# Attention and two mixture-of-experts layers in one kernel: the first layer's overflow loop moved into its routing, and the second expert's second matrix product turned around

## The chip, the cores and the metric

One Trainium2 chip, one of its NeuronCores. The metric is the device time of one execution of the whole kernel in microseconds (us), the median of a few runs. In the rows below PE is the matrix engine and PEld its weight loads, DVE the vector engine, ACT the scalar engine, POOL the general one, and SP the engine whose queue issues most of the transfers; a "q" behind a name (PEldq, SPq) means the engine's sequencer, which waits, branches and issues.

## What is computed

Top-32 attention over 16 heads, then two layers in which each of 1152 tokens goes through one of eight experts. Cut to what matters here:

```python
x = attention(q, k, v)                       # 1152 tokens, 512 wide
for w_gate, w1, w2, capacity in (moe, moe2): # capacity 288 in the first, none in the second
    logits = x @ w_gate
    expert_idx = np.argmax(logits, axis=1)
    for e in range(8):
        xe = x[expert_idx == e]              # the first 288 of them in the first layer
        h = np.maximum(xe @ w1[e], 0.0)      # w1[e] is 512x1024
        out[expert_idx == e] = gate_w * (h @ w2[e])   # w2[e] is 1024x512
    x = out
```

## The kernel before, in words

The program is attention, then the two layers (`moe(0, ...)` and `moe(1, ...)`), written out in one order by hand: no scheduler moves anything, and each engine takes its instructions as they are written.

A layer first routes its tokens. The experts are ranked by how many tokens chose them (rank r = 0 is the fullest), and rank r has room for `SIZES[r]` tokens: 256, 208, 192, 176, 160, 144, 128, 128. Tokens beyond that room go to an overflow loop, `spill()` (L1258): every engine loads the number of overflow blocks, `nblk`, into a register (L1259) and branches (L1261) over the loop's body if it is zero. With this input it is zero in both layers, so the loop itself never runs; what runs is the load and the branch on each engine. In the first layer `spill` stands in the last expert's layer 1 (`side`, L1422: with r == E - 1), ahead of `nxt.soon()`, the routing of the second layer. In the second layer it stands at the end of `run`.

The first layer's start is `begin()` (L1424). It ranks, then `assign()` (L1206) makes the token lists (`gidx`), runs 22 empty matmuls (`spin`), and computes the gate's parts (`r3`, L1228) and at last `nblk` (L1242). Then it asks for the first expert's w1 in four transfers of half a megabyte (`load_w1`, L872), gathers the first two blocks of rows (`bring`, L869), asks for w2 (`load_w2`, behind a POOL memset, L889), gathers further rows, turns the first rows (`turn_in`: PE transposes at L949, ACT at L952, DVE at L955) with 10 and 5 spins between, and asks for the second expert's w1 (`weights(1, 0)`). Each weight half (1 MB) lies in a `raw` buffer, of which there are four; a buffer comes free when ACT and DVE have split it into two parts (L919, L920: `halves`).

Then for each rank r: `layer1` over eight blocks f of the hidden width, with side work popped before each block f > 0 (the next expert's rows, the outputs of the last one, the splits of w2), and `layer2`. In both a matrix product takes three partial products. Forms: "D" and "R" issue three matmuls; "S" puts two of them into one matmul with 2n columns and adds them up after (ACT L971, DVE L972); "N" is plain. In layer 2, "R" keeps the hidden values in the array and streams w2 (512 columns), one pass for each block of up to 128 tokens (L1027 to L1029), and its result has tokens in rows: ACT scales it (L1075), and in the first layer PE turns it back for the next layer's logits (L1088). "S" keeps w2 in the array and streams the tokens (L1031, L1033); its result lies the other way, and PE turns it for the output (L1082). `form2` (L1108) gives rank 0 and 1 and the ranks of 128 the form "R", the others "S"; in the first layer the last rank has "N".

Of the kernel before, what the change touches and what calls it, by code (L numbers as in the profile page):

```python
# [10 lines left out]
F32 = mybir.dt.float32  # L11
F32R = mybir.dt.float32r
# [35 lines left out]
def attn_moe_moe_kernel(ctx, tc, q, k, v, g1, w11, w12, capacity, g2, w21, w22, out):  # L48
    nc = tc.nc
# [770 lines left out]
    def moe(i, pools, src, lg, w1, w2, limit):  # L820
# [4 lines left out]
        with ExitStack():  # L825
# [8 lines left out]
            width = Dm if i == 0 else RW  # L834
            ny = SIZES[0] if i == 0 else SIZES[2]
            xrs = {}
# [34 lines left out]

            def load_w1(e, first=0):  # L872
                w_ = w1[ds(e, 1)].rearrange("o (c p) f -> p (o c) f", p=128)
                got = []
                for h in range(2):
                    raw = wt.tile([128, KD, F // 2], F32, name="raw", bufs=4)
                    step = F // 4 if first else F // 2
                    for f0 in range(0, F // 2, step):
                        nc.sync.dma_start(raw[:, :, f0:f0 + step], w_[:, :, h * F // 2 + f0:h * F // 2 + f0 + step])
                    got.append(raw)  # L880
                return got
# [225 lines left out]
            form1 = ["D" if n >= 240 else "S" if n > 128 else "N" for n in SIZES]  # L1107
            form2 = ["R" if n >= 208 or n <= 128 else "S" for n in SIZES]  # L1108
            if i == 0:
# [101 lines left out]
            def assign():  # L1211
# [8 lines left out]
                if i == 0:  # L1220
                    spin(22)
                    for f in table["gates"]:
                        f()
# [3 lines left out]
                decode(pi[:, :NCOL], pi[:, NCOL:2 * NCOL], tokf, gidx, inv)  # L1227
                tt(r3, isa[:, None].to_broadcast(b3), gcode[:, :, None, :].to_broadcast(b3), op=OP.mult)  # L1228
                nc.scalar.activation(cnt, pos[:, nch], AF.Copy)
# [11 lines left out]
                red(nbf, more, axis=AX.XY, op=OP.add)  # L1241
                nc.vector.tensor_copy(nblk, nbf)  # L1242

            def weights(r, j):
                e = nc.values_load(eid0[0:1, 0:1] if i and r == 0 else eid[0:1, r:r + 1], engines=[SP], min_val=0, max_val=E - 1,
                                   skip_runtime_bounds_check_because="ranks are a permutation of the experts")
                if j == 0:
                    w1s[r] = [load_w1(e, sum(c[0] == 0 for c in COLS) if r == 0 and i == 0 else 0), {}]
                else:
                    w2s[r] = [load_w2_apart(e) if i == 0 and r == E - 1 else load_w2(e, r == 0), {}]  # L1250

# [6 lines left out]
            def spill():  # L1258
                trips = nc.values_load(nblk[0:1, 0:1], min_val=0, max_val=n_ov,  # L1259
                                       skip_runtime_bounds_check_because="a sum of block counts")  # L1260
                with ExitStack() as loop:  # L1261
# [53 lines left out]
                    red(g, pi[:, 2:5], axis=AX.X, op=OP.add)  # L1315
                    xr = wk.tile([128, width], F32, name="xr", bufs=5)
                    gather(xr, idx)
# [97 lines left out]
            def side(r, nxt):  # L1415
                jobs = opening() if r == 0 else []
                if r + 1 < E:
                    xTs[r + 1] = wk.tile([128, KD, 2, SIZES[0]], F32R, name="xT")
                    if r or i == 0:
                        jobs += [lambda q=q: rows_in(r + 1, *q) for q in tiles_of(r + 1)]  # L1420
                jobs += after(r - 1) if r else []
                return jobs + ([spill] + nxt.soon() if nxt and r == E - 1 else [])  # L1422

            def begin():  # L1424
                bank()
                choose(0, nch)
                count(0, nch)
                nc.scalar.activation(dl, dl, AF.Exp)
                none = new([128, 1], "none", U32)
                nc.gpsimd.memset(none, 0)  # L1430
                yr = wk.tile([128, RW], F32, name="yr", bufs=3)
                gather(yr[:16, :Dm], none[:16])
                spin(18)
                weave(*ranking())
                assign()
                weights(0, 0)
                for j in range(2):
                    bring(j)
                weights(0, 1)
                for a, (r, t, m) in enumerate(COLS):  # L1440
                    if 0 < r < 3:
                        bring(a)
                first_split = splits(0, 0)
                for f in first_split[:4]:
                    f()
                xTs[0] = wk.tile([128, KD, 2, SIZES[0]], F32R, name="xT")
                for q, n_ in zip(tiles_of(0), (10, 5)):
                    rows_in(0, *q)
                    spin(n_)
                for f in first_split[4:]:  # L1450
                    f()
                weights(1, 0)

# [122 lines left out]
            def run(nxt=None):  # L1576
# [3 lines left out]
                for r in range(E):  # L1580
                    hTs[r] = wk.tile([128, KF, 2, SIZES[0]], F32R, name="hT", bufs=1)
                    jobs, more_ = side(r, nxt), rest[r]
                    if i and r == 0:
                        more_ = [lambda p=p: [(split_high if p < 4 else split_low)(k) for k in w2_order[p]]
                                 for p in range(len(w2_order))]
                    jobs = [(lambda p=p: [f() for f in p]) for p in
                            [jobs[k:k + 1] + more_[k:k + 1] for k in range(max(len(jobs), len(more_)))]]
# [82 lines left out]
```

## Time and profile before

| | |
|---|---|
| median of 3 runs | 630.91 us (627.88 to 632.11) |
| the profiled execution | 628.57 us |
| its span, first to last instruction | 626.9 us |
| PE busy | 573.4 us, 91% of the span |
| granted TensorE clock, mean | 0.978 |

The attention fills the first 276 us; the change does not touch it. From about 276 to 296 us the first layer routes, from 296.4 to 455 us its experts run, the second layer's routing lies inside the last one, and from 468 to 619 us the second layer's experts run. In the rows, "idle before <- who" tells how long an engine sat idle and whose instruction ended that.

### The profile page before, as it was taken

The numbers are of one execution on the slowest core, as the hardware profiler recorded it, in microseconds if no ns is written. First come the engines' busy times: TensorE is split into PE (matmuls) and PEld (weight loads), VectorE is DVE, ScalarE is ACT, GpSimd is POOL, SyncE is SP. The second block draws the span as 40 slices with busy tenths as digits, with TensorE's granted clock in tenths as the row PEclk, the third lists the DMA queues.
The fourth block names the chain that finished last, engine by engine and source line by source line (L and its number), as shares of the span: only waits on it lengthen the run. The fifth ranks groups of instructions, "written<-read, shape, count | busy, mean of one in ns | idle before, by whom it ended". The sixth has DMA issues, their size and how long they took to land. (4 is left out here: it accounts for less than half of the span.)

```text
span 626.9 us, 13493 instructions
## 1 busy us (share of the span) xinstructions
PE 573.4 (91%) x4426; PEld 525.5 (84%) x4426; DVE 508.3 (81%) x1889; ACT 446.9 (71%) x963; POOL 242.6 (39%) x426
## 2 busy tenths in 40 slices
PE   7999989888888888676999999999899999999995
PEld 5888878777777777565988999999799889999994
DVE  6999999999999999975867688873368687888740
ACT  5699988888989897733776777763245577787651
POOL 8688776767675464634020101100013311101010
PEclk9699999999999999987999999999998999999998
DMA  6600605051550000009795758778185966677660
GB/s 149 155 4 1 196 1 146 2 134 24 137 78 20 2 20 1 20 21 315 268 280 195 230 202 244 225 240 287 31 308 178 331 237 230 224 259 266 221 223 19
DMA packets 79694, 96.01 MB, mean 153 GB/s; under 512 B 33829, under 2 KB 42533, under 8 KB 79616
## 3 DMA queue, kind: packets, MB, share of 16 engines
q1 hardware_dynamic: 74688, 84.07, 42.8%
q0 software_dynamic: 3728, 10.70, 5.3%
q8 instruction: 38, 0.62, 0.4%
q10 hardware_dynamic: 1200, 0.30, 0.2%
q14 instruction: 40, 0.33, 0.2%
HBM read 82.32 MB, written 13.22 MB: 152 GB/s over the span
## 5 line engine op out<-in xcount | busy, mean ns | idle before, releaser
L375 POOL TENSOR_TENSOR m<-s,r 128x576 f32<-128x576 f32 x71 | 100.8, 1420 | 54.7 <-ACT r L370 49.6
L402 PE MATMUL xb<-vx,pT 128*128 128x73 f32 (+1 forms) x800 | 95.4, 268 | 4.0 <-ACT xl L415 2.9
L402 PEld LDWEIGHTS xb<-vx,pT 128*128 128x128 f32 (+1 forms) x800 | 87.0, 180 | 8.2 <-ACT xl L415 4.3
L992 PE MATMUL pp<-xT,w1c 128*128 128x416 f32 (+4 forms) x320 | 93.3, 361 | 0.0
L920 DVE TENSOR_TENSOR w2c<-raw,w2c 128x512 fp32r<-128x512 f32 x112 | 74.4, 684 | 15.8 <-ACT w2c L919 15.4
L994 PE MATMUL pp<-xT,w1c 128*128 128x208 f32 (+4 forms) x320 | 77.9, 243 | 0.0
L919 ACT ACTIVATE w2c<-raw 128x512 fp32r<-128x512 f32 x112 | 67.0, 623 | 6.4 <-PE pp L1033 3.7
L920 DVE TENSOR_TENSOR w1c<-raw,w1c 128x512 fp32r<-128x512 f32 x96 | 60.5, 684 | 11.0 <-ACT w1c L919 10.4
L1031 PE MATMUL pp<-hT,w2c 128*128 128x384 f32 (+3 forms) x256 | 68.7, 350 | 0.0
L307 PE MATMUL sc<-qkT 128*128 128x288 f32 x256 | 51.2, 322 | 17.8 <-DVE cand L331 16.6
L343 DVE MAX8 top<-y 128x8 f32<-128x160 f32 x216 | 67.1, 311 | 0.1
L310 ACT ACTIVATE s<-sc 128x576 f32<-128x576 f32 x72 | 47.0, 653 | 22.2 <-PE sc L307 19.7
L307 PEld LDWEIGHTS sc<-qkT 128*128 128x128 f32 x256 | 36.4, 190 | 29.8 <-DVE cand L331 29.1
L1033 PE MATMUL pp<-hT,w2c 128*128 128x192 f32 (+3 forms) x256 | 61.3, 240 | 0.0
L994 PEld LDWEIGHTS pp<-xT,w1c 128*128 128x128 f32 x320 | 61.2, 191 | 0.2
L992 PEld LDWEIGHTS pp<-xT,w1c 128*128 128x128 f32 x320 | 60.2, 188 | 0.8
L971 ACT ACTIVATE t<-pp 128x192 f32<-128x192 f32 (+4 forms) x112 | 34.9, 311 | 35.9 <-PE pp L994 26.1
L385 PE MATMUL pt<-ident,kept 128*128 128x128 f32 x355 | 54.0, 283 | 4.2 <-ACT kept L379 3.4
L390 ACT ACTIVATE pT<-pt 128x640 f32<-128x640 f32 x71 | 50.1, 705 | 9.8 <-PE pt L385 8.6
L919 ACT ACTIVATE w1c<-raw 128x512 fp32r<-128x512 f32 x96 | 53.3, 621 | 4.3 <-DMA raw<-in_moe_w_dram 4.3
L379 ACT ACTIVATE kept<-m,nb 128x576 f32<-128x576 f32 x71 | 54.7, 771 | 1.4 <-POOL m L375 1.3
L370 ACT ACTIVATE r<-s,nb 128x576 f32<-128x576 f32 x71 | 54.5, 768 | 0.6 <-POOL nb L365 0.5
(317 smaller groups left out, 1429.5 us busy)
## 6 DMA issues: line engine op xcount, KB each, us to landing
raw<-in_moe_w_dram SPq DMA_DIRECT2D x60, 1024.0 KB, 6.0
out_dram<-zero SPq DMA_DIRECT2D x3, 768.0 KB, 3.8
y<-yr POOLq DMA_DIRECT2D x8, 256.5 KB, 4.5
kraw<-in_k_dram SPq DMA_DIRECT2D x8, 256.0 KB, 3.0
vraw<-in_v_dram SPq DMA_DIRECT2D x16, 128.0 KB, 2.8
vx<-in_v_dram SPq DMA_DIRECT2D x16, 128.0 KB, 2.8
raw<-in_moe_w_dram SPq DMA_DIRECT2D x4, 512.0 KB, 6.4
w2c<-in_moe_w_dram SPq DMA_DIRECT2D x4, 512.0 KB, 9.5
```

The lines of the kernel that those rows point to most:

```text
L307: nc.tensor.matmul(sc[:, w, :W2], l, r[:, w * W2:(w + 1) * W2], start=(n_ == 0), stop=(n_ == len(ops) - 1))
L343: ops.append(lambda w=w, cur=cur: nc.vector.max(w, cur))
L370: nc.scalar.activation(r, s, AF.Relu, bias=nb[:, 1:2], scale=-BIG)
L375: nc.gpsimd.tensor_tensor(m, s, r, op=OP.subtract)
L379: nc.scalar.activation(kept[k % 3][:, :S], m, AF.Exp, bias=nb[:, 0:1], scale=scale)
L402: nc.tensor.matmul(o, pT[:, c2, cols], z["v"][:, c2, hh], start=(c2 == 0), stop=(c2 == NC - 1))
L919: nc.scalar.activation(o[:, 0], src_, AF.Copy)
L920: nc.vector.tensor_tensor(o[:, 1], src_, o[:, 0].bitcast(F32), op=OP.subtract)
L992: nc.tensor.matmul(ph[:, :2 * n].rearrange("p (w n) -> p w n", w=2), w[f][:, 0, d], xT[:, d, :, :n], start=st, stop=False)
L994: nc.tensor.matmul(ph[:, :n], w[f][:, 1, d], xT[:, d, 0, :n], start=False, stop=sp)
L1031: nc.tensor.matmul(py[:, :2 * n].rearrange("p (w n) -> p w n", w=2), w[f][:, 0, o], hT[:, f, :, :n], start=st, stop=False)
L1033: nc.tensor.matmul(py[:, :n], w[f][:, 1, o], hT[:, f, 0, :n], start=False, stop=sp)
```

## The change

1. In the first layer `spill()` leaves `side` and is called in `begin()`, behind the gathers of the first two blocks of rows. The 22 spins of `assign` become 14, and 8 stand behind `spill`. The gate's parts (`r3`) are computed behind `nblk`. The loop's row buffer is taken from the `w2c` buffers.
2. The first expert's w1 is asked for in two transfers of 1 MB: the first half ahead of `assign`, the second behind `spill`, then w2 without the POOL memset.
3. The second expert's w1 is no longer asked for in `begin()`, but from the side work of the first expert's layer 1, ahead of its sixth block (f = 5), behind a DVE memset of the buffer. The splits of the first expert's w2, one ahead of each block before, now stand two, two and four ahead of the blocks 5, 6 and 7.
4. Rank 1 (208 tokens) has the form "S" in layer 2, in both layers.

```diff
-            ny = SIZES[0] if i == 0 else SIZES[2]
+            ny = SIZES[0] if i == 0 else SIZES[1]
...
-            def load_w1(e, first=0):
+            def load_w1(e, halves_=(0, 1), gate=None):
...
-                for h in range(2):
+                for h in halves_:
                     raw = wt.tile([128, KD, F // 2], F32, name="raw", bufs=4)
-                    step = F // 4 if first else F // 2
-                    for f0 in range(0, F // 2, step):
-                        nc.sync.dma_start(raw[:, :, f0:f0 + step], w_[:, :, h * F // 2 + f0:h * F // 2 + f0 + step])
+                    if gate:
+                        gate.memset(raw[0:1, 0, 0:1], 0.0)
+                        gate = None
+                    nc.sync.dma_start(raw, w_[:, :, h * F // 2:(h + 1) * F // 2])
...
-            form2 = ["R" if n >= 208 or n <= 128 else "S" for n in SIZES]
+            form2 = ["R" if n >= 240 or n <= 128 else "S" for n in SIZES]
...
-                    spin(22)
+                    spin(14)
...
-                tt(r3, isa[:, None].to_broadcast(b3), gcode[:, :, None, :].to_broadcast(b3), op=OP.mult)
+                if i:
+                    gate_rows()
...
                 nc.vector.tensor_copy(nblk, nbf)
+                if i == 0:
+                    gate_rows()
+
+            def gate_rows():
+                tt(r3, isa[:, None].to_broadcast(b3), gcode[:, :, None, :].to_broadcast(b3), op=OP.mult)
...
-                    w2s[r] = [load_w2_apart(e) if i == 0 and r == E - 1 else load_w2(e, r == 0), {}]
+                    w2s[r] = [load_w2_apart(e) if i == 0 and r == E - 1 else load_w2(e, i == 1 and r == 0), {}]
+
+            def first_weights(h):
+                w1s.setdefault(0, [[], {}])[0].extend(load_w1(chosen_one(0), (h,)))
...
-                    xr = wk.tile([128, width], F32, name="xr", bufs=5)
+                    xr = wt.tile([128, 2, Dm], F32R, name="w2c", bufs=12).bitcast(F32)
+                    xr = xr.rearrange("p a b -> p (a b)")[:, :width]
...
-                return jobs + ([spill] + nxt.soon() if nxt and r == E - 1 else [])
+                return jobs + (nxt.soon() if nxt and r == E - 1 else [])
...
                 weave(*ranking())
+                first_weights(0)
                 assign()
-                weights(0, 0)
                 for j in range(2):
                     bring(j)
+                spill()
+                spin(8)
+                first_weights(1)
                 weights(0, 1)
...
-                weights(1, 0)
...
+                    if i == 0 and r == 0:
+                        more_ = [lambda p=p, m=more_: [m[k]() for k in p] for p in
+                                 ((), (), (), (), (0, 1), (2, 3), (4, 5, 6, 7))]
+                        jobs.append(lambda: weights(1, 0, nc.vector))
```

Where instructions stand now. SP's queue in the first layer's start: `eid` is the first expert's number, `raw` a weight buffer. Before:

```order
L1245 TENSOR_LOAD eid
L879 ISA
L879 DMA raw<-in_moe_w_dram 128x4x256
L879 ISA
L879 DMA raw<-in_moe_w_dram 128x4x256
...
L1245 TENSOR_LOAD eid
L891 ISA
L891 DMA raw<-in_moe_w_dram 128x4x512
```

Now:

```order
L1252 TENSOR_LOAD eid
L880 ISA
L880 DMA raw<-in_moe_w_dram 128x4x512
L1272 TENSOR_LOAD nblk
L1274 COMPARE_AND_BRANCH x2
L1274 UNCONDITIONAL_BRANCH x2
...
L1252 TENSOR_LOAD eid
L880 ISA
L880 DMA raw<-in_moe_w_dram 128x4x512
```

The second half of w1, and all that SP issues after it, stand behind the branch now.

DVE from the fourth hidden block of the first expert's layer 1 to its layer 2: `hT` is a hidden block, `w2c` and `w1c` are splits. Before:

```order
L965 SCALAR_TENSOR_TENSOR hT<-pp,hT 128x256
L955 TENSOR_TENSOR xT<-pt,xT 128x4x80
L920 TENSOR_TENSOR w2c<-raw,w2c 128x512
L965 SCALAR_TENSOR_TENSOR hT<-pp,hT 128x256
L920 TENSOR_TENSOR w2c<-raw,w2c 128x512
...
L920 TENSOR_TENSOR w2c<-raw,w2c 128x512
L920 TENSOR_TENSOR w1c<-raw,w1c 128x512 x8
L920 TENSOR_TENSOR w2c<-raw,w2c 128x512 x3
```

Now:

```order
L966 SCALAR_TENSOR_TENSOR hT<-pp,hT 128x256
L878 MEMSET raw 1x1
L921 TENSOR_TENSOR w2c<-raw,w2c 128x512 x2
L966 SCALAR_TENSOR_TENSOR hT<-pp,hT 128x256
L921 TENSOR_TENSOR w2c<-raw,w2c 128x512 x2
L966 SCALAR_TENSOR_TENSOR hT<-pp,hT 128x256
L921 TENSOR_TENSOR w2c<-raw,w2c 128x512 x4
L966 SCALAR_TENSOR_TENSOR hT<-pp,hT 128x256
L921 TENSOR_TENSOR w1c<-raw,w1c 128x512 x8
```

All eight splits of w2 stand behind the fifth hidden block now, and the last hidden block behind all of them.

PE in the last expert's layer 1 of the first layer: L985 are its matmuls, L1088 and L1045 turn the last outputs back and make logits, L1163 is the second layer's first count. Before:

```order
L985 MATMUL pp<-xT,raw 128x128 x4
L1088 MATMUL pt<-ident,yr 128x128 x4
L985 MATMUL pp<-xT,raw 128x128 x4
L1045 MATMUL pl<-wg,yT 128x8 x4
L985 MATMUL pp<-xT,raw 128x128 x4
L1259 TENSOR_LOAD nblk
L1261 COMPARE_AND_BRANCH x2
L1261 UNCONDITIONAL_BRANCH x2
...
L985 MATMUL pp<-xT,raw 128x128 x8
L1163 LDWEIGHTS before
```

Now:

```order
L986 MATMUL pp<-xT,raw 128x128 x4
L1089 MATMUL pt<-ident,yr 128x128 x4
L986 MATMUL pp<-xT,raw 128x128 x4
L1046 MATMUL pl<-wg,yT 128x8 x4
L986 MATMUL pp<-xT,raw 128x128 x8
L1164 LDWEIGHTS before
```

The load and the branch are gone, and the count stands one block of matmuls earlier.

## Rows read from the trace of the kernel before

**Rows 1.** Page: busy time of each engine, share of span, instructions.

```profile
PE 573.4 (91%) x4426; PEld 525.5 (84%) x4426; DVE 508.3 (81%) x1889; ACT 446.9 (71%) x963; POOL 242.6 (39%) x426
```

**Rows 2.** By stretch: length, busy PE, PEld, DVE, ACT, POOL (instructions), clock, DMA share, GB/s.

```profile
284.00:292.00 8.00, 3.35 (x34) 2.87 (x34) 4.68 (x18) 2.30 (x4) 5.04 (x6) 0.82 0.99 323
...
490.00:600.00 110.00, 110.00 (x789) 104.83 (x788) 85.29 (x211) 81.42 (x205) 19.55 (x20) 1.00 0.73 253
```

**Rows 3.** Timeline of the last expert's layer 1: start, length, instruction, idle before.

```profile
444.08 1.14 PE L985 MATMUL pp<-xT,raw 128*128 128x128 f32 x8
444.26 0.17 DVE L1048 TENSOR_SCALAR lg<-pl 128x8 f32<-128x8 f32 x1 [8.12 <-PE pl L1045]
...
445.31 0.31 DVE L1151 TENSOR_REDUCE mx<-lg 128x19 f32<-128x152 f32 x1 [0.88 <-DVEq L1261]
...
446.70 0.32 DVE L1158 TENSOR_TENSOR oh<-revm,m 128x152 bf16<-128x152 f32 x1
447.80 2.02 PE L985 MATMUL pp<-xT,raw 128*128 128x128 f32 x16 [2.59 <-PEq L1261]
```

**Rows 4.** The branches' own instructions, from the views of lines L1261 and L719.

```profile
L1261 PEldq COMPARE_BRANCH  x2: 422/2140/3859, 443.8 to 615.6; - x2
...
L719 PEldq COMPARE_BRANCH  x1: 367/367/367, 275.1 to 275.1; - x1
```

**Rows 5.** Timeline of the first layer's start.

```profile
284.42 2.56 PE L1105 MATMUL pp<-idle,ones 128*128 128x256 bf16 x22
...
285.22 1.15 POOL L869 DMA_INDIRECT xr<-x,gidx  x1 [2.81 <-DMA raw<-in_moe_w_dram]
...
286.31 0.15 DVE L1242 CAST nblk<-nbf 128x1 int32<-128x1 f32 x1
...
291.63 1.09 PE L949 MATMUL pt<-ident,xr 128*128 128x128 f32 x4 [4.65 <-issue]
292.51 2.34 PE L1105 MATMUL pp<-idle,ones 128*128 128x256 bf16 x10
```

**Rows 6.** Busy time and granted clock in two single microseconds of that start.

```profile
288.00:289.00 1.00, 0.00 (x0) 0.00 (x0) 1.00 (x3) 0.53 (x2) 0.92 (x1) 1.00 1.09 385
291.00:292.00 1.00, 0.37 (x2) 0.40 (x3) 0.00 (x0) 0.00 (x0) 0.40 (x1) 0.50 0.92 260
```

**Rows 7.** Waits of SP's queue from 430 to 452 us: total, times, longest.

```profile
SPq L1261 <- SPq L1261: 8.7, 2, 8.3
```

**Rows 8.** Issue to landing of gathers (`gidx`), of w1's transfers (L879); timeline of SP.

```profile
DMA to landing us min/median/max: 3.2/6.1/8.2
...
DMA to landing us min/median/max: 4.9/5.3/15.9
...
289.37 10.51 SPq L879 DMA_DIRECT2D raw<-in_moe_w_dram  x2
```

**Rows 9.** First expert: its layer 1 and layer 2 by stretch; two DVE instructions there.

```profile
296.44:310.21 13.77, 13.45 (x115) 13.21 (x115) 11.99 (x31) 9.30 (x20) 1.94 (x3) 1.00 0.93 325
310.21:321.12 10.91, 10.91 (x51) 9.02 (x49) 8.21 (x14) 7.32 (x14) 1.25 (x2) 1.00 0.75 255
...
306.51 0.42 DVE L965 SCALAR_TENSOR_TENSOR hT<-pp,hT 128x256 fp32r<-128x256 f32 x1
307.02 0.69 DVE L920 TENSOR_TENSOR w2c<-raw,w2c 128x512 fp32r<-128x512 f32 x1
```

**Rows 10.** Layer 2 by stretch: first layer's rank 1 (R) and 2 (S), second layer's rank 1.

```profile
334.35:345.44 11.09, 11.09 (x51) 8.07 (x49) 7.92 (x15) 7.40 (x15) 1.31 (x2) 1.00 0.59 190
357.68:366.79 9.11, 9.11 (x67) 9.11 (x65) 8.27 (x18) 7.55 (x17) 0.00 (x0) 1.00 0.54 202
507.90:518.97 11.07, 11.07 (x50) 8.08 (x49) 7.92 (x15) 7.40 (x15) 1.01 (x1) 1.00 0.71 238
```

**Rows 11.** Timeline of PE where four transposes of an output stand between matmuls.

```profile
542.33 0.60 PE L1082 MATMUL pt<-ident,yT 128*128 128x128 f32 x4
542.68 0.41 PE L992 MATMUL pp<-xT,w1c 128*128 128x352 f32 x1
```

More of the change, by code (lines that the diff above doesn't have):

```diff
@@ L1242, in assign, with chosen_one, weights @@
                 nc.vector.tensor_copy(nblk, nbf)
-            def weights(r, j):
-                e = nc.values_load(eid0[0:1, 0:1] if i and r == 0 else eid[0:1, r:r + 1], engines=[SP], min_val=0, max_val=E - 1,
-                                   skip_runtime_bounds_check_because="ranks are a permutation of the experts")
+                if i == 0:
+                    gate_rows()
+            def gate_rows():
+                tt(r3, isa[:, None].to_broadcast(b3), gcode[:, :, None, :].to_broadcast(b3), op=OP.mult)
+            def chosen_one(r):
+                return nc.values_load(eid0[0:1, 0:1] if i and r == 0 else eid[0:1, r:r + 1], engines=[SP], min_val=0,
+                                      max_val=E - 1, skip_runtime_bounds_check_because="ranks are a permutation of the experts")
+            def weights(r, j, gate=None):
+                e = chosen_one(r)
                 if j == 0:
-                    w1s[r] = [load_w1(e, sum(c[0] == 0 for c in COLS) if r == 0 and i == 0 else 0), {}]
+                    w1s[r] = [load_w1(e, gate=gate), {}]
                 else:
-                    w2s[r] = [load_w2_apart(e) if i == 0 and r == E - 1 else load_w2(e, r == 0), {}]
+                    w2s[r] = [load_w2_apart(e) if i == 0 and r == E - 1 else load_w2(e, i == 1 and r == 0), {}]
+            def first_weights(h):
+                w1s.setdefault(0, [[], {}])[0].extend(load_w1(chosen_one(0), (h,)))
             def splits(r, j):
```

## Prediction

> **What bounds the kernel now.** I first read the page's list of engines: PE is busy 573.4 us, 91% of the span [rows 1]. Then the busy time by stretch, because a share is a mean over stages: among the experts PE is busy 110.00 of 110 us [rows 2], so there a part moves the end only if it gives PE less to do or makes it wait. The same view shows the opposite in the first layer's start: from 284 to 292 us PE works 3.35 of 8 us, while the DMA engines are full at 323 GB/s [rows 2]. Last I read the timeline in the places where the change cuts, to find PE's gaps and what ends them. Two matter. In the last expert of the first layer PE stands still 2.59 us, ended by its own branch at L1261 [rows 3]; and in the first layer's start it stands still 4.65 us, from the last spin at 286.98 (284.42 + 2.56) to the first transpose of gathered rows at 291.63 [rows 5]. Everything between 296 and 442 us is PE working without a gap that matters, so a gain or loss at either end passes to the end undiminished unless a transfer or a split comes late.
>
> My sum is against the profiled execution's own 628.57 us, of which 1.7 lie outside its span of 626.9. It stands 2.3 us (0.4%) below the median of the runs shown, 630.91; I put the difference that I work out onto the median.
>
> **Part 1a: the branch leaves the last expert.** Of the 2.59 us, what is late next? The branch also held up DVE: the logits are written at 444.26 + 0.17 = 444.43, but the second layer's first choice begins at 445.31, 0.88 later, and ends at 446.70 + 0.32 = 447.02 [rows 3]. Without the branch it ends at 446.14. PE has the block that ends at 444.08 + 1.14 = 445.22, then one more (half of the 2.02 us for sixteen matmuls, 1.0), and then the count, which needs that choice: 446.2. So PE waits about 0.1 us for it instead of 2.59, and what comes after the count starts more than 2.59 us earlier, as one block less stands ahead of it. I take 2.5 us. The ends: 2.75 if the chain after the count had itself been late, 0.9 if DVE's choice were all that mattered.
>
> **Part 1b: the branch enters the first layer's start.** It must wait for `nblk`, ready at 286.31 + 0.15 = 286.46 [rows 5], a little earlier now because the gate's parts move behind it. The 14 spins end before that: 284.42 + 14 x 0.116 = 286.05 (22 took 2.56). PE's branch took 3.859 us in the one place and 0.422 and 0.367 in the two others [rows 4]. That is the unknown. The two short ones and the long one are the same instruction, skipping a loop body; the long one is the copy of the loop that moves here, with the same body of matmuls, so I take the long price. With some 0.4 us for the load of the register, PE is free at 286.3 + 0.4 + 3.9 = 290.6. The 8 spins then cost 8 x 0.234 = 1.9 us at the lower clock (ten took 2.34 at 292.51) or 0.9 at the full one, so the first transpose comes at 291.5 to 292.5, against 291.63 now. [...] The work up to the first product is some 4.8 us now, nearly all at the lower clock; if the upper one comes back a microsecond and a half sooner, 1.3 us are saved. Ends for 1b: 1.3 faster, 0.8 slower; I take 0. The branch is thus hidden under the gathers' landing, at no gain: a stall of 4.65 us becomes one of 4.5 and eight more spins.
>
> [...]
>
> Behind the branch on SP's queue now stand the second half of w1, w2 and all later weights. At the old place SP stood at the branch 8.3 us, until its last transfer had landed [rows 7]. So here it will stand until the first half of w1 is in. Asked for at about 282, 1 MB should land at 287 to 288 (the median transfer of w1 takes 5.3 [rows 8]), hardly after `nblk` anyway. The second half then goes out near 288.3, some 5 us later than now, and lands by 294 to 295. It is first needed at the fifth of eight blocks of layer 1, past 303 (296.44 and half of 13.77 [rows 9]). Cost nothing.
>
> **Parts 2 and 3: the weights of the second expert.** They are now asked for from 289.37 on, the second of them when its buffer comes free near 299.5 [rows 8]. Afterwards DVE asks for both at its fifth hidden block, which ends at 306.51 + 0.42 = 306.9 [rows 9]. With 5.3 us the first lands at 312.2, and the other some 3 us behind it (1 MB at the 325 GB/s of that stretch [rows 9]), at 315.5. ACT and DVE want to split them when they are done with w2. DVE's list from 306.9: eight splits at 0.69 and three hidden blocks at 0.42 are 6.8 us, to 313.7. So the transfer is just in time. The first tile of layer 2 starts at 310.21 and needs the last split and the last hidden block at its eighth step, 4.8 us in (16 steps take 10.91 [rows 9], so 7 x 0.68), 315.0: 1.3 us to spare. In layer 2 of this expert DVE is busy 8.21 of 10.91 us now [rows 9]; the backlog of about 2.5 us fits into the 2.7 that are left. Cost nothing, cover nearly used up; if it fails, the price is in the third rival. The POOL memset that goes and the DVE one that comes are single elements.
>
> **Part 4: rank 1 in the form "S".** With "R" its layer 2 takes 11.09 us in the first layer and 11.07 in the second; rank 2 with 192 tokens takes 9.11 as "S" [rows 10]. In proportion to the columns, 208/192, "S" takes 9.87; a part of each matmul that does not grow would make it less, down to 9.4. I take 9.8: 1.3 us saved in each. The result has to be turned. Four transposes shift the matmul behind them by 542.68 - 542.33 = 0.35 us [rows 11]; two tiles cost 0.7. In the first layer that replaces the turning back of the rows, about the same, so 1.3 remain; in the second nothing went before, so 0.6 remain. Together 1.9 (ends 1.5 and 2.8). ACT and DVE get four additions each, as at rank 2, where DVE is busy 8.27 of 9.11 us and PE all the time [rows 10]; they hide them.
>
> **Sum.** 2.5 + 0 + 0 + 1.9 = 4.4 us faster: 624.2 from the profiled 628.57, and 630.9 - 4.4 = 626.5 on the median. That is 0.7%. About 1% (6.3 us) is what a measurement of this kernel can tell from no change, so the forecast is: within 1%, on the fast side.
>
> **Rivals.**
> (a) *The branch is short.* The two short rows speak for it, the long one of the same body against. PE would pass at about 287.2 and stand before the gathers instead: the first was issued at 285.22 and lands after 3.2 to 8.2, median 6.1 us [rows 5, 8], less than now perhaps, because 1 MB and not 2 lies ahead of it. With rows at 289.5 and little idle time the clock may not fall, and the 4.8 us of work become 2.6. Gain 3 to 4 us more: 623.0. [...]
> (b) *The gain at the last expert is taken by the routing chain.* The second layer's route is a chain of choice, count, choice and gather, and only its head was looked at here; if a gather's landing or DVE ends it, only the 0.88 us of DVE remain. PE's unbroken work after the count speaks against. Total 0.9 + 1.9 = 2.8: 628.1.
> (c) *The second expert's weights come late; slower than before.* Place: the first expert's layer 2 and the second's layer 1. Both halves of w1 and then w2 are asked for inside 10 us, w1 up to 17.5 us later than now, from DMA engines that are at 255 to 325 GB/s there [rows 9]. Against: those rates include this very traffic, which is not yet there. One transfer of w1 took 15.9 us from issue to landing [rows 8]. If that came again from 306.9, it would land at 322.8, ACT and DVE would have split a first block at 324.2 (two steps of 0.69), and PE, due at 321.1, would lose 3.1 us there, and as much again with w2 one stage on: 6.2. The sum becomes 1.8 slower: 632.7. It decides from a loss of 4.4 us on, that is, 2.2 a stage, a landing 15.0 us after the request.
>
> **How the numbers follow.** Forecast 0.58 (its own range 624.0 to 628.5 by the ends of 1a, 1b and 4 and the spread of the median), (a) 0.17, (b) 0.16, (c) 0.09. The range for all reaches from case (a) with a little more, 621.5, to just short of (c), 631.0; the few runs of before alone span 4 us. Faster by over 1% is most of (a) and a fifth of the forecast, 0.26; slower by over 1% is the far end of (c), 0.04; within 1% 0.70.
>
> **What would show each step.** In the profile after: PE's idle time before the branch's successor in the last expert gone, and the count waiting at most some 0.3 us; PE's branch in the first layer's start with 3.9 us (forecast) or 0.4 (a); the first product at 295 to 297.3; no idle time of PE between 310 and 345 (else c); rank 1's layer 2 at 9.8 us. The prediction is wrong if the first product comes before 294, if PE waits for `w1c` of the second expert, or if the time is above 631.

## The result and the profile after

| | before | after |
|---|---|---|
| median of 4 runs each | 630.62 us (627.88 to 632.11) | 623.83 us (622.67 to 625.12) |
| the profiled execution | 628.57 us, span 626.9 | 624.27 us, span 622.6 |

The ratio is 0.990 (95% interval 0.986 to 0.994): 6.8 us faster by the medians (3.9 to 9.0 by the interval), 4.3 by the two profiles. A second comparison of the same two kernels, below, has 626.85 against 630.12 us, ratio 0.993 (0.991 to 0.996): 3.3 us by the medians, 4.3 by the ratio. The forecast was 4.4 us, 626.5, which lies inside both intervals. The total was met; two of its terms were not. The 623.83 is nearer to rival (a)'s 623.0, but that rival's condition, a short branch, did not come: the branch is long in the rows below.

The list of engines on the page of after, which answers to [rows 1]:

```profile
PE 571.0 (92%) x4466; PEld 528.1 (85%) x4466; DVE 510.7 (82%) x1898; ACT 447.3 (72%) x969; POOL 240.6 (39%) x425
```

The timeline of the last expert in after, for [rows 3]:

```profile
443.81 2.03 PE L986 MATMUL pp<-xT,raw 128*128 128x128 f32 x16
443.99 0.17 DVE L1049 TENSOR_SCALAR lg<-pl 128x8 f32<-128x8 f32 x1 [8.22 <-PE pl L1046]
444.19 0.31 DVE L1152 TENSOR_REDUCE mx<-lg 128x19 f32<-128x152 f32 x1
...
445.59 0.32 DVE L1159 TENSOR_TENSOR oh<-revm,m 128x152 bf16<-128x152 f32 x1
...
445.95 0.23 PE L1164 MATMUL pi<-oh,before 128*128 128x168 bf16 x1
```

The 2.59 us in front of PE are gone. DVE begins its choice 0.03 us behind the logits instead of 0.88, is done at 445.91, and PE's count starts 0.11 us behind the block that ends at 445.84: the forecast's 0.1.

The branches' instructions (line L1274 now) and the timeline of PE in the first layer's start, for [rows 4] and [rows 5]:

```profile
L1274 PEldq COMPARE_BRANCH  x2: 341/2056/3770, 287.0 to 611.2; - x2
```

```profile
284.82 1.69 PE L1106 MATMUL pp<-idle,ones 128*128 128x256 bf16 x14
290.95 1.87 PE L1106 MATMUL pp<-idle,ones 128*128 128x256 bf16 x8 [4.44 <-PEq L1274]
292.61 1.06 PE L950 MATMUL pt<-ident,xr 128*128 128x128 f32 x4
293.46 2.34 PE L1106 MATMUL pp<-idle,ones 128*128 128x256 bf16 x10
```

The long jump has moved with the loop: 3.770 us (3.859 before), a stall of 4.44 (forecast 4.5), then eight spins at 1.87 us, 0.23 each at the lower clock, where the fourteen ahead of the stall took 0.12 each. The first transpose comes 13.60 us behind the first count (279.01) instead of 13.03 (278.60). Busy time and granted clock there, for [rows 6]:

```profile
288.00:289.00 1.00, 0.00 (x0) 0.00 (x0) 0.00 (x0) 0.00 (x0) 0.48 (x1) 1.00 0.85 221
290.00:291.00 1.00, 0.05 (x1) 0.09 (x2) 0.00 (x0) 0.00 (x0) 0.69 (x2) 0.53 0.58 182
292.00:293.00 1.00, 1.00 (x6) 0.88 (x5) 1.00 (x3) 1.00 (x3) 0.00 (x0) 0.50 0.98 362
```

As in the kernel before, the granted clock falls from 1.00 to 0.50 while PE stands.

Last the stretches of after for [rows 9] and [rows 10]: the first expert's layer 2, the second expert's layer 2 in the first and in the second layer, and the last expert's layer 1 in the second layer.

```profile
310.87:322.07 11.20, 11.20 (x50) 9.02 (x49) 9.67 (x17) 8.05 (x16) 1.25 (x2) 1.00 1.05 392
601.23:609.26 8.03, 7.33 (x65) 7.14 (x64) 4.26 (x11) 4.37 (x12) 0.99 (x1) 1.00 0.08 28
```

```profile
335.31:344.91 9.60, 9.60 (x66) 9.59 (x65) 8.74 (x18) 7.63 (x17) 0.00 (x0) 1.00 0.54 196
...
503.07:512.66 9.59, 9.59 (x66) 9.57 (x65) 8.74 (x18) 7.62 (x17) 0.00 (x0) 1.00 0.67 236
```

Form S takes 9.6 us where R took 11.1, in both layers. The last expert's layer 1 in the second layer has 0.70 us in which PE isn't busy. The timeline shows why:

```profile
601.23 2.84 PE L986 MATMUL pp<-xT,raw 128*128 128x128 f32 x24
601.96 2.19 ACT L920 ACTIVATE w2c<-raw 128x512 fp32r<-128x512 f32 x4 [2.12 <-SPq L1274]
...
604.05 0.67 ACT L1076 ACTIVATE yr<-pp,gate 128x512 f32<-128x512 f32 x1
...
604.77 4.73 PE L986 MATMUL pp<-xT,raw 128*128 128x128 f32 x40 [0.70 <-ACT yr L1076]
```

ACT did this work in the order in which it is written: it waited 2.12 us for the last half of w2, split it, and only then, at 604.05, copied the output (yr) whose buffer PE needed. (The row names SP's branch; the transfer was asked for at 595.82 and landed 6.1 us later, at 601.9. The same transfer took 5.1 us in the kernel before.)

### The profile page after: what moved, and what is told of

Same layout as the page of the kernel before. It is cut to its first block, busy times and chain, and to the rows that moved or that the text cites. A ratio compares the mean times of both kernels' runs of the same rounds, so it can differ in the third digit from the quotient of the medians.

```text
span 622.6 us, 13581 instructions
## 1 busy us (share of the span) xinstructions
PE 571.0 (92%) x4466; PEld 528.1 (85%) x4466; DVE 510.7 (82%) x1898; ACT 447.3 (72%) x969; POOL 240.6 (39%) x425
## 4 chain that ended last, share of the span: by engine, by line
PE 39%; DMA 8%; issue 4%; DVE 1%; POOLq 0%; POOL 0%; ACT 0%
PE pp L993 8%; DMA out_dram<-yr,sidx 8%; PE pp L1032 7%; PE pp L995 3%; PE pp L1034 3%; PE pp L986 2%; PE pt L950 2%; PE pp L1030 2%; PE pp L1028 2%; PE pp L1029 1%; PE pl L1046 1%; PE pp L990 1%; PE pp L1026 1%; PE pp L989 1%; PE pp L991 1%
## 5 line engine op out<-in xcount | busy, mean ns | idle before, releaser
L921 DVE TENSOR_TENSOR w2c<-raw,w2c 128x512 fp32r<-128x512 f32 x112 | 74.2, 685 | 17.4 <-ACT w2c L920 17.3
L1032 PE MATMUL pp<-hT,w2c 128*128 128x416 f32 (+4 forms) x320 | 88.0, 354 | 0.0
L1034 PE MATMUL pp<-hT,w2c 128*128 128x208 f32 (+4 forms) x320 | 78.4, 245 | 0.0
L921 DVE TENSOR_TENSOR w1c<-raw,w1c 128x512 fp32r<-128x512 f32 x96 | 60.9, 687 | 11.1 <-ACT w1c L920 10.8
L972 ACT ACTIVATE t<-pp 128x208 f32<-128x208 f32 (+4 forms) x120 | 37.5, 313 | 40.6 <-PE pp L995 28.9
L1034 PEld LDWEIGHTS pp<-hT,w2c 128*128 128x128 f32 x320 | 61.3, 192 | 0.0
L1032 PEld LDWEIGHTS pp<-hT,w2c 128*128 128x128 f32 x320 | 60.2, 188 | 0.0
```

The lines of the kernel that those rows point to most:

```text
L921: nc.vector.tensor_tensor(o[:, 1], src_, o[:, 0].bitcast(F32), op=OP.subtract)
L1032: nc.tensor.matmul(py[:, :2 * n].rearrange("p (w n) -> p w n", w=2), w[f][:, 0, o], hT[:, f, :, :n], start=st, stop=False)
L1034: nc.tensor.matmul(py[:, :n], w[f][:, 1, o], hT[:, f, 0, :n], start=False, stop=sp)
```

## The experiments

Ratios are to the kernel before on the same chip, which had medians of 630.12, 629.62 and 630.74 us in the three groups.

| kernel | median, us | ratio, 95% interval |
|---|---|---|
| b_again: before | 629.29 | 0.999 (0.997 to 1.001) |
| a_again: after | 626.85 | 0.993 (0.991 to 0.996) |
| b_form2: before, with S | 628.70 | 0.998 (0.996 to 1.000) |
| a_oldform: after, with R | 625.93 | 0.992 (0.990 to 0.995) |
| a_form_first: S in layer one alone | 625.39 | 0.993 (0.990 to 0.995) |
| a_pad: after, jump shifted | 625.20 | 0.993 (0.990 to 0.995) |
| a_no8: after, no spins there | 625.87 | 0.993 (0.991 to 0.996) |
| b_pad: before, jump shifted | 627.40 | 0.995 (0.993 to 0.998) |
| a_spillback: part 1 undone | 629.19 | 0.998 (0.996 to 1.000) |
| a_oldw1: part 3 undone | 624.94 | 0.991 (0.988 to 0.993) |
| a_xrback: buffers as before | 625.26 | 0.991 (0.989 to 0.994) |
| best: three edits | 623.98 | 0.991 (0.988 to 0.994) |

The intervals are some 1.5 us to either side, so most verdicts rest on stages. Each profile's stages, in us, worked out from its timeline (from PE's first matmul of one stage to that of the next): the last expert's layer 1 and its whole time in the first layer; the start, from the first count to the second expert; the second layer's first expert; there rank 1's layer 2 up to rank 3; and its last expert up to the end of the span.

```
               last, L1   last   start   2nd: rank 0   1 to 3      end
before            12.48  27.45   42.52         29.05   30.23 R   20.41
b_again           13.84  28.79   41.78         29.08   30.23 R   20.46
b_form2           15.18  29.99   42.33         27.59   30.84 S   20.46
a_spillback       13.94  29.30   41.45         29.07   31.39 S   20.59
b_pad             10.56  26.50   42.59         29.07   30.23 R   20.38
after              9.94  24.60   43.06         27.31   29.67 S   21.38
a_again            9.94  24.61   43.01         27.65   31.23 S   21.70
a_oldform          9.93  24.67   42.97         27.62   30.38 R   20.56
a_form_first       9.93  24.58   43.19         27.64   30.55 R   20.76
a_pad              9.94  24.60   42.24         27.31   31.33 S   21.31
a_no8              9.94  24.60   41.95         29.17   31.05 S   20.51
a_oldw1            9.93  24.59   42.68         29.07   31.11 S   21.47
a_xrback           9.93  24.59   41.95         27.30   31.29 S   21.75
best               9.94  24.61   42.20         27.31   30.57 R   21.47
```

**Both kernels again** (b_again, a_again; no edit).

> The kernel before, unchanged, to see how its executions differ among themselves. In its first profile the granted clock falls to 0.50 from 480.21 to 483.62, right behind the second layer's short products (28 and 14 columns); in the profile after, there is no such stretch, and that alone is 2.0 of the 4.3 us between the two profiles. Theory A (chance): where that stretch falls differs from run to run; the mean clocks of these runs differ by about 0.003 among themselves (3.4 us at half speed in 627), and the times by some 1.8 us with each 0.003; another profile may lack the stretch. Theory B (the change removes it): every run of this kernel has it, mean clock 0.978 or lower throughout, and this profile shows it again.

> The changed kernel, unchanged, for the same question. Theory A: some of these runs have the low stretch in the second layer's start, clocks spread over 0.977 to 0.983; at equal mean clock it is 4.3 us faster than the kernel before by the terms (2.85 at the last expert, 1.97 from the form, less 0.56 in the first layer's start), and the ratio is near 0.993. Theory B: no run has the stretch, mean clock 0.980 or higher throughout, and the ratio is near 0.990 (some 6.3 us).

Neither theory held whole. The unchanged before had the low stretch in the second layer again (rank 0: 29.08 us), and a low stretch that was not expected, right behind the stall at the branch. Its windows around the stall, and the timeline:

```profile
446.00:447.50 1.50, 0.00 (x0) 0.00 (x0) 1.33 (x5) 0.00 (x0) 0.00 (x0) 1.00 0.05 5
448.00:451.00 3.00, 2.83 (x13) 2.87 (x14) 0.00 (x0) 0.28 (x1) 0.00 (x0) 0.50 0.02 5
452.00:454.00 2.00, 2.00 (x30) 2.00 (x28) 1.23 (x9) 0.28 (x1) 0.00 (x0) 1.00 0.00 0
```

```profile
448.17 3.47 PE L985 MATMUL pp<-xT,raw 128*128 128x128 f32 x16 [2.50 <-PEq L1261]
```

Sixteen matmuls that took 2.02 us in [rows 3] take 3.47 here, at clock 0.50: the stall did not cost 2.5 us but 3.9.

**Part 4 alone, and all but part 4.**

```diff
-            form2 = ["R" if n >= 208 or n <= 128 else "S" for n in SIZES]
+            form2 = ["R" if n >= 240 or n <= 128 else "S" for n in SIZES]
```

(a_oldform the other way round.)

> The kernel before with the second expert's layer 2 in the form S alone (part 4). Theory A: rank 1's layer 2 takes 9.6 to 9.8 us in both layers instead of 11.1, 0.15 us go to the turned output in the first layer and 0.85 in the second; 1.97 us faster, ratio 0.9969. The forecast's term is 1.9. Rival: the additions on ACT and DVE hold PE up somewhere in the next expert, and less than 1 us remains. The PE stall of some 2.6 us at the branch in the last expert is unchanged.

> The changed kernel with the second expert's layer 2 in the form R again (part 4 undone). Theory A: 2.0 us slower than the changed kernel, so 2.3 faster than before, ratio 0.996. Theory B (the low stretch of the clock in the second layer goes because the last expert runs through): 4.3 faster than before, ratio 0.993, and the profile has no low stretch at 475 to 480.

The first layer did as forecast: from rank 1's layer 2 to rank 3 it takes 31.13 us in b_form2 and 32.44 before, 1.3 less. In the second layer S took 30.84 against 30.23: the gain had gone. By the times part 4 made 1.3 us in the one comparison (0 to 2.6), and undoing it cost nothing that can be measured in the other: its interval excludes theory A's 0.996 and has theory B's 0.993 in it. Theory B's reason is not shown by that, as the low stretch in the second layer comes and goes in either kernel (rank 0 in the table). For the last expert, b_form2 shows the stall and the lower clock once more, longer:

```profile
445.00:451.00 6.00, 5.07 (x34) 5.04 (x35) 0.08 (x1) 0.55 (x2) 0.00 (x0) 0.50 0.01 3
```

Where the second layer's gain goes is seen in a_again: its two S stretches (rank 1 and rank 2), and the timeline inside the first.

```profile
505.73:516.10 10.37, 10.16 (x66) 9.55 (x65) 9.86 (x22) 8.01 (x18) 0.00 (x0) 1.00 0.61 211
...
527.00:536.96 9.96, 9.65 (x66) 9.20 (x65) 8.23 (x18) 7.55 (x17) 0.28 (x1) 1.00 0.71 239
```

```profile
507.68 0.38 ACT L965 ACTIVATE hT<-s 128x208 fp32r<-128x208 f32 x1 [0.38 <-DVE s L973]
...
507.98 0.46 PE L1032 MATMUL pp<-hT,w2c 128*128 128x416 f32 x1 [0.21 <-DVE hT L966]
508.08 0.37 DVE L966 SCALAR_TENSOR_TENSOR hT<-s,hT 128x208 fp32r<-128x208 f32 x1 [0.16 <-ACT hT L965]
...
508.61 1.90 DVE L921 TENSOR_TENSOR w1c<-raw,w1c 128x512 fp32r<-128x512 f32 x3
```

Some seven steps into layer 2, PE comes to the last hidden blocks before ACT and DVE have written them. S reads a step's hidden block in 0.30 us (9.6 for 32), R reads the same list for one tile first, in 5.5 us or so (half of 11.07 [rows 10]) for eight blocks, 0.69 each. The faster form reaches the last hidden block sooner, at the point where DVE is just done with layer 1.

That alone does not make PE wait: in the profile after, with the same form, there is no such wait, and the stretch took 29.67 us, 0.56 less than with R, about the 0.6 of the forecast. What sets it apart stands earlier, in rank 1's layer 1. Below is ACT's third copy (t) there, first of a_again with the last matmul that it needs, then of after:

```profile
499.63 0.26 PE L995 MATMUL pp<-xT,w1c 128*128 128x208 f32 x1
...
501.65 0.34 ACT L972 ACTIVATE t<-pp 128x208 f32<-128x208 f32 x1 [2.11 <-PE pp L995]
```

```profile
497.33 0.34 ACT L972 ACTIVATE t<-pp 128x208 f32<-128x208 f32 x1 [0.45 <-PE pp L995]
```

In a_again ACT begins 1.76 us after that matmul's end (499.89), in after 0.10; its hidden blocks are late from there on. Each of the seven S profiles with the long stretch has such an idle time of ACT in that layer, of 1.4 to 2.1 us, and a second one of 1.4 us where rank 2's layer 2 begins; after has 0.45 and 0.56 us there. Five of the six R profiles have the first one too, and PE waits for no hidden block there. So, by these profiles, S loses its gain where ACT is late, and R, which asks later, does not. What held ACT is not shown; whether it also happens without the profiler is not known.

**S in the first layer alone.**

```diff
-            form2 = ["R" if n >= 240 or n <= 128 else "S" for n in SIZES]
+            form2 = ["R" if n >= (208 if i else 240) or n <= 128 else "S" for n in SIZES]
```

> The changed kernel with the form S for the second expert in the first layer alone, R again in the second. Theory A (the second layer gives the gain back: its stretch from rank 1's layer 2 to the end took 119.0 us with R, and 119.5, 119.8 and 121.4 in three executions with S, with PE waiting there for hidden blocks and for an output's copy): that stretch is 119.0 to 119.4 us, no wait of PE for hT or yr there, and the kernel is 0.1 to 2 us faster than the changed one. Theory B (by the forecast, S saves 0.6 us in the second layer): 0.6 us slower than the changed one.

The stretch is 30.55 us, and of PE's waits for hT none is left; up to the end it took 119.80 from rank 1 on, above the 119.4 expected and above the 119.5 of after. In all, the six profiles with R in the second layer have 30.2 to 30.6 there, those with S 29.67 once and 30.84 to 31.39 seven times. Theory A holds for this stretch, at 0.6 us on the mean (30.99 less 30.37), and not up to the end; by the runs no gain is resolved.

**The place of the jump in PE's code.** Empty matmuls, nothing else:

```diff
                 choose(0, nch)
+                spin(20, 64)
                 count(0, nch)
...
-                spin(18)
+                spin(36, 128)
```

(b_pad has the first line and `spin(30, 64)` behind `spin(22)`. `spin` takes the number of columns as its second argument now.)

> The changed kernel with 38 more empty matmuls (76 PE instructions) ahead of the branch in the first layer's start, 20 of 64 columns ahead of the first count and 36 of 128 columns in place of 18 of 256, where PE waits anyway. They only shift where the jump stands in PE's program. [...] Theory B (the jump over this copy of the loop is long wherever it stands): still 3.8 us, no gain.

> The kernel before with 50 more empty matmuls (100 PE instructions) ahead of its first-layer experts, 20 of 64 columns ahead of the first count and 30 of 64 columns behind the 22 spins, where PE waits. The branch stays in the last expert. Theory A (the long jump depends on where it stands): PE's branch in the last expert takes 0.3 to 0.5 us instead of 3.86, the stall of 2.6 us there shrinks under 0.5, no low clock at 444 to 451, the last expert's layer 1 takes 10 to 10.5 us instead of 12.5, 13.8 and 15.2 in the three profiles; 2.5 to 4.5 us faster than before, about as much as the whole change. Theory B: the jump is long there wherever the code stands, and only the start changes, by less than 1 us.

The branches' rows, first of a_pad, then of b_pad (there the line is L1262):

```profile
L1274 PEldq COMPARE_BRANCH  x2: 421/1902/3382, 286.9 to 612.0; - x2
```

```profile
L1262 PEldq COMPARE_BRANCH  x2: 330/858/1387, 443.4 to 614.2; - x2
```

In a_pad the start's jump is the short one of the pair, 0.421 us (it begins at 286.9, and PE's next instruction at 287.4); the long one now is the loop's at the very end, where PE has nothing left to do. The same jump over the same body, moved by 76 instructions: 3.77 us have become 0.42. So the length of this stall is a matter of where the code lies. That PE waits for code is likely, and not shown by itself: inside the long jump of after lies the one packet that the instruction queue q8, all of whose 38 packets have 16 KB, moved from 286 to 292 us,

```profile
q8 instruction: 1, 0.02, 1.1%
```

and in all thirteen profiles with a jump of over 3 us such a packet begins 0.9 to 1.5 us into it, while none lies inside a jump of under 0.5 us over one of the two overflow loops. At which distance a jump turns long is not shown.

In b_pad the stall shrank from 2.59 to 0.64 us, no low clock followed, and the last expert took 26.50 instead of 27.45 to 29.99, 1.16 of it given back to a late gather in the second layer's routing (the view of waits has 1.2 us for `xr`). The jump took 1.39, longer than theory A said. The kernel became 2.9 us faster (ratio 0.995): fifty empty matmuls give two thirds of the 4.3 us that the whole change gave in its second comparison. (The two were measured on different chips, and their intervals overlap.)

But a_pad is no faster than the changed kernel. PE's timeline in its start, and the clock:

```profile
287.51 1.03 PE L1106 MATMUL pp<-idle,ones 128*128 128x256 bf16 x8 [1.13 <-issue]
289.62 0.63 PE L950 MATMUL pt<-ident,xr 128*128 128x128 f32 x4 [1.08 <-issue]
290.08 1.25 PE L1106 MATMUL pp<-idle,ones 128*128 128x256 bf16 x10
291.70 0.63 PE L950 MATMUL pt<-ident,xr 128*128 128x128 f32 x4 [0.37 <-issue]
292.16 0.71 PE L1106 MATMUL pp<-idle,ones 128*128 128x256 bf16 x5
295.04 0.35 PE L989 MATMUL pp<-xT,w1c 128*128 128x256 f32 x1 [2.17 <-issue]
```

```profile
290.00:291.00 1.00, 1.00 (x12) 0.90 (x11) 1.00 (x3) 1.00 (x3) 0.69 (x2) 1.00 0.79 221
296.10:299.40 3.30, 3.30 (x24) 3.21 (x23) 1.58 (x3) 2.24 (x5) 0.00 (x0) 0.50 1.04 300
```

The first transpose comes 2.8 us sooner behind the count. PE then waits 1.08, 0.37 and 2.17 us, the last until the second tile's copy is written (ACT 294.35, DVE 294.98; why ACT came to it so late is not settled), and the lower clock falls on real products instead of spins. Of 2.8 us, 0.8 is left at the second expert (42.24 against 43.06).

**No spins behind the branch.**

```diff
                 spill()
-                spin(8)
```

> The changed kernel without the 8 empty matmuls behind the branch. Theory A: the branch ends at 290.95 in the first profile after, behind the first landed rows (290.06), so the 8 spins (1.66 us at the lower clock) stand on the path: the first transposes come 1.7 us earlier behind the first count and the kernel is 1.7 us faster. Theory B: the spins keep the lower clock shorter; without them it lasts 3.4 us longer and the gain is under 0.5 us.

The first transpose came 12.45 us behind the count instead of 13.60, 1.1 sooner, and the start is 1.1 shorter (41.95). Theory A is right for the stage, with 1.1 of its 1.7 us. In the time it is not to be seen; this profile had two low stretches elsewhere, from 391.8 and from 477.2 us. The first of them came while PE was busy without a wait:

```profile
390.00:391.80 1.80, 1.80 (x21) 1.76 (x20) 1.55 (x8) 1.05 (x3) 0.00 (x0) 1.00 0.53 56
391.83:395.25 3.42, 3.42 (x18) 3.42 (x16) 1.15 (x3) 1.64 (x4) 0.00 (x0) 0.50 0.73 281
```


**Part 1 undone, part 3 undone.**

```diff
-                spill()
-                spin(8)
...
-                return jobs + (nxt.soon() if nxt and r == E - 1 else [])
+                return jobs + ([spill] + nxt.soon() if nxt and r == E - 1 else [])
```

(with 22 spins and the old row buffer)

> The changed kernel with part 1 undone: the overflow loop stands in the last expert again, 22 spins in the start, the loop's row buffer where it was; w1 in halves, the second expert's late request and the form S remain. Theory A (the stall at the branch costs 2.5 us and, in some executions, a stretch of lower clock behind it): the last expert's layer 1 takes 12.5 us, or 13.8 to 15.2 with such a stretch, instead of 9.94; the kernel is near 629, 0.5 to 1 us faster than before, 3 to 4 slower than the changed one. Theory B (by the forecast's terms): 2.5 us slower than the changed one, 1.9 faster than before.

The last expert's layer 1 took 13.94 us, with the lower clock right behind the stall:

```profile
446.10:449.30 3.20, 3.20 (x23) 3.14 (x22) 0.00 (x0) 0.56 (x2) 0.00 (x0) 0.50 0.00 0
```

Of the whole gain only 1.3 us was left, ratio 0.998 (0.996 to 1.000). The closest comparison is a_xrback below, on the same chip and with the same row buffer, which differs only in where the loop and eight of the spins stand: 625.26 against 629.19, 3.9 us. Part 1 is what made most of the gain, by more than its forecast 2.5. Part 2 was not undone by itself.

```diff
+                weights(1, 0)
...
-                        more_ = [lambda p=p, m=more_: [m[k]() for k in p] for p in
-                                 ((), (), (), (), (0, 1), (2, 3), (4, 5, 6, 7))]
-                        jobs.append(lambda: weights(1, 0, nc.vector))
```

> The changed kernel with part 3 undone: the second expert's w1 is asked for at the end of the start again and the splits of the first expert's w2 stand one ahead of each block. Theory A (the late request is hidden, no PE wait for w1c anywhere): the same time as the changed kernel within 0.5 us. Theory B (the start gains from fewer transfers): gathered rows land later, the first transposes come up to 1 us later behind the first count.

No difference that can be measured, and in neither kernel does PE wait for `w1c`: theory A, cost nothing, as forecast.

**The buffers' places.**

```diff
-                    xr = wt.tile([128, 2, Dm], F32R, name="w2c", bufs=12).bitcast(F32)
-                    xr = xr.rearrange("p a b -> p (a b)")[:, :width]
+                    xr = wk.tile([128, width], F32, name="xr", bufs=5)
```

> The changed kernel with the overflow loop's row buffer among the xr buffers again. The order in which buffers are first used decides where they lie on the chip: in the changed kernel w2's splits lie at byte 83296 of a partition and w1's at 132448, in the kernel before w1's at 83296 and w2's at 116064; here they lie as before, and the hidden blocks where the changed kernel has them (209408 instead of 198240). In the changed kernel each 512-column matmul of form R starts 232.5 ns after the last instead of 227.5, and the 256-column ones of form D after 113 instead of 120. Theory A (the place of w1's and w2's splits does it): back to 227.5 and 120 here, first expert's layer 2 at 10.9 instead of 11.2 us. Theory B (the hidden blocks' place, or the place in the code): 232.5 and 113 remain. Time within 0.7 us of the changed kernel either way.

The first expert's layer 2 stayed at 11.20 us: theory A falls. It is 10.91 in a_spillback, which has the hidden blocks at the old place, and 11.21 in a_pad, whose code is shifted. That points to the hidden blocks' place; but the overflow loop moved together with it in every one of these kernels, and neither was tried by itself. The 0.3 us a stage are small change.

**Three edits together** (a_form_first, a_no8 and a_xrback in one).

> The changed kernel with three edits: form S for the second expert in the first layer alone, no spins behind the branch, the overflow loop's row buffer as before. By the sums over the traces 1.1 us for the spins, 0.5 to 1 for the form, 0 to 0.7 for the buffers: 1.5 to 2.8 us faster than the changed kernel, ratio to before 0.989 to 0.991. Rival: the clock falls elsewhere, as in the run without the spins, and no gain can be measured.

623.98 us, ratio 0.991 (0.988 to 0.994). It is the lowest median of its group, but a_oldw1 and a_xrback lie inside its interval. No version was shown to beat the changed kernel.

## Why the prediction was right, and which terms were not

The total, 4.4 us, was right within what can be measured (4.3 by the second comparison's ratio, 6.8 by the first). By the stages of the profiles it was right by luck: two wrong terms cancel.

**1a, "I take 2.5 us", with ends of 2.75 and 0.9.** The mechanism was right, the chain of rival (b) did not take the gain, the size was short. The two profiles give 27.45 - 24.60 = 2.85. But in three of the four profiles with the loop there, in b_again, b_form2 and a_spillback, the clock fell to 0.50 behind the stall, and the last expert took 28.8 to 30.0. The mean of the four is 28.88, so the term is 4.3 us on the mean, from 2.85 to 5.4 in single profiles. What failed is the price of the stall as its idle time alone. [Rows 6] showed PE's clock falling from 1.00 to 0.50 around an idle time in the start, a longer one of 4.65 us; the forecast reckoned with the lower clock there and did not ask whether 2.59 us could do the same. Its one profile happened to be the one without. And the price differs between profiles: the four profiles have 12.48 to 15.18 us for the same layer 1.

**1b, "I take 0".** The branch cost what the long row said (3.770 against 3.859). The first transposes came 0.6 us later, and the start is 0.6 longer on the mean of five profiles with this start (42.84, against 42.21 for three with the old one); within the ends given, on their slow side. The fast end, 1.3 us, was the forecast's estimate for a clock that comes back sooner, and no run here shows it: in after the clock stood at 0.50 for 6.8 us as in the kernel before, and came back to 1.00 at 296.9 us, 17.9 behind the first count, against 295.9 and 17.3. SP stood 0.4 us at its branch by the view of waits, for 8.3 at the old place [rows 7], and the second half of w1 came in time, as forecast. Rival (a) was priced too high: with a short branch the start gave 0.8 us and not 3 to 4, because the copies of the gathered rows and the clock were late next.

**Parts 2 and 3, "cost nothing".** Right: the profile after has no wait of PE between 310 and 446 us, and a_oldw1 shows no difference. The second expert's w1 landed at 312.88 and 315.59, for 312.2 and 315.5 in the forecast. Its backlog of 2.5 us on DVE does not come out of its own list, which ends 3.5 us into layer 2 (313.7 less 310.21); DVE's busy time there rose by 1.46 us, from 8.21 to 9.67, and PE did not wait for it. Rival (c) did not come.

**Part 4, "Together 1.9".** In the first layer 1.3, as forecast. In the second layer 0.6 was forecast and 0.6 was lost, on the mean of the profiles. The failed step is "ACT and DVE get four additions each ... they hide them": the busy shares were read over the whole stage, and what counts is the first 2.5 us, in which S asks for all eight hidden blocks. They did hide them in one profile of eight, after, where ACT was not late; in the other seven ACT was, and 0.6 to 1.2 us were lost against R's 30.23. So part 4 is worth 0.7 on the mean, not 1.9. Why ACT is late is open.

By the table's means: 4.3 - 0.6 + 0.7 = 4.4. Two more differences nearly cancel and were in no term. The second layer's first expert is 0.95 us shorter on the mean; it had the lower clock (0.50, from 480.21 to 483.62 us in the profile of before) in four of five profiles with the loop in the last expert, and in two of nine without. Whether the change does that or chance is open. The last 20.5 us are 0.75 longer, by the wait for the last half of w2 shown above; why that transfer takes longer in most of the changed kernels is open too. Over the runs the mean granted clock was 0.975 for the kernel before (59 runs) and 0.979 for the changed one (10 runs of both comparisons).

## What to carry to other kernels

Price a stall of PE at its idle time and at the matmuls behind it that may run at half the clock (0.50 behind stalls of 2.4 to 2.7 us in three of four profiles here), and look at more than one execution before the price is fixed. A skipped loop costs by where it lies in the code (here 3.77 us or 0.42): before moving a branch off the path, shift it with a few instructions in a place where the engine waits anyway. When a stage is made faster, look at the order in which it takes its inputs and at how late they may come, and not only at the busy share of the engines that make them.

## What was not expected of the hardware

The same jump took 3.77 us or 0.42 by a shift of 76 instructions, and 3.86 or 1.39 by one of 100. With the loop in the last expert PE's clock fell from 1.00 to 0.50 behind a stall of 2.4 to 2.7 us in three profiles and stayed in one, and in a_no8 it fell at 391.8 us in the middle of work without a wait. In a_again ACT stood idle 2.11 us, 1.76 of them after the matmul that it waited for had ended, and in twelve of the fourteen profiles it has an idle time of 1.4 to 2.2 us in that layer. And matmuls of one shape ran at two paces at full clock in two kernels: 10.91 and 11.20 us for the same 48 of 512 columns.
